# Four-step exponential, kv stage on GpSimd, 128-column q/k blocks and a four-offset convolution: one change to a fused convolution and attention kernel

## Chip, cores and metric

The kernel runs on one core of a Trainium2 chip. The metric is device time in microseconds (us), one launch per time. Lower is better. A time of a kernel that ran once has no state ("unknown"); where a kernel ran several times, a run over 1.5% above its fastest counts as slow, and ratios use the fast runs.

## The reference, cut to what matters

Two independent halves share the core; S = 2048, D = 640, bf16.

```python
# half A: short convolution, product, long causal convolution, gate
k_shift = sum over t of k_pad[:, t:t + S, :] * shift_k[:, 3 - t]
kv = k_shift * v
y = causal convolution of kv with ssm_k, length 2048, per channel   # by FFT in the reference
a = q * (y + kv * ssm_D)

# half B: attention, 32 heads of 20
qkv = x @ wqkv
p = softmax((q @ k.T) * 20 ** -0.5)
b = (p @ v) @ wo
out = concatenate([a, b], axis=-1)
```

## The kernel before

A Python planner writes one static program. It holds a clock per engine, adds an assumed cost `c` for every instruction and decides from those clocks what TensorE (PE) does next. The work is 2,048 *units* of 128x512 scores: a matmul of 20 rows writes a unit into a bank of PSUM, an exponential turns it into a tile of `P_sb`, a second matmul multiplies that by v. ScalarE (ACT) takes two or three units per instruction (a *round*); VectorE (DVE) takes single units by a bit trick.

```python
def EXP_task(k, m, vec, b0, got):              # m = 2 or 3 units
    ...
    P.op("act", lambda e: e.activation(
        P_sb[:, s0:s0 + m, :],
        PS[:, b0 * 512:(b0 + m) * 512].rearrange("p (u q) -> p u q", u=m), ACT.Exp, scale=scale),
        ...
    if vec:
        chain_start(k + m, b0 + m, got[m])

# chain_start: five DVE steps; the PSUM bank is free after the first
(lambda e: e.tensor_scalar(XI, bank[bk], scale * 1.4426950408889634 * w, 127.0 * w, op0=ALU.mult,
                           op1=ALU.add), [bkb[bk]], [bl, bh], 0.691, False),
(lambda e: e.scalar_tensor_tensor(XZ, u, w * c2 / c3, u, op0=ALU.add, op1=ALU.mult), [bl], [bz], 0.69, True),
(lambda e: e.tensor_scalar(hi, hi, 128.0, None, op0=ALU.mult), [bh], [bh], 0.456, True),
(lambda e: e.scalar_tensor_tensor(XZ, XZ, w * w * c1 / c3, u, op0=ALU.add, op1=ALU.mult), ...),
(lambda e: e.scalar_tensor_tensor(P_sb[:, z, :].bitcast(U16), XZ, 128.0 * c3 / w ** 3, hi, ...), ...)
```

The long convolution is 5,120 small matmuls (a block Toeplitz form): 16 distances `d` of 128 positions, and 8 to 128 columns in each.

```python
for d in range(16):
    for r1 in range(2):
        n = (16 - d) * 4
        ...
        lhsT = HK[sl][:, 64 + 128 * d - 32 * r1:64 + 128 * d - 32 * r1 + 128]
        rhs = sub(KVX[i], [[128, 2], [1, n]], ql * 256 + r1 * 64)     # 2n columns
        ...
        cost = max(0.025, 2 * n / 2400 + 0.0025)
```

The last thing that the planner tries when it has nothing else for PE is to multiply zeros. `P.stream` holds what PE *streams*, that is columns divided by 2.4 a nanosecond, not how long it looks busy:

```python
while P.stream and P.stream[0][0] < now - 3.4:
    P.stream.pop(0)
if sum(x[1] for x in P.stream) < ZTH and slack > 0.45 and bnow > 1:      # ZTH = 1.8
    if 0 < npv[0] % NKB:
        zeros(OBANK, 2, False)          # two matmuls of 512 zero columns
        continue
    ...
```

So zeros are added when less than 1.8 of the last 3.4 us, a share of 0.53, were streaming. Transfers are issued from SyncE; the planner books 0.43 us for each:

```python
return self.op(eng, fn, reads, writes, dsem=dsem, n=len(pairs), c=0.43 * len(pairs), kb=kb)
```

The softmax here doesn't subtract the row's maximum and nothing guards it: scores larger than these inputs give would overflow.

## Time and profile before

| | before |
|---|---|
| time, median of the first 3 runs | 893.01 us (890.0 to 896.05) |
| span of the profiled run, mean granted clock | 889.3 us, 0.987 |
| exponentials: ACT rounds of three / of two, DVE units | 419 / 310, 171 |
| convolution matmuls | 5,120, from 232.5 to 829.3 us |

The prediction shows the lines that tell what bounds it. Three more matter for what came of it: the row of the granted clock (40 slices of the span, 9 is 90% of full speed or more), the group of zero matmuls (busy us, mean ns, then the idle time before them), and ACT's wait for PE (us in all, times, longest).

```profile
PEclk9999999999699999999999999999999999999999
```

```profile
L348 PE MATMUL PS<-Zt 128*128 128x512 bf16 x208 | 63.6, 402 | 1.5 <-DVE Zt L342 1.0 <-DVE R L952 0.5
```

```profile
ACT P_sb L639 <- PE PS L597: 18.4, 24, 7.0
```

The clock is full in every slice but one. 208 zero matmuls are part of what keeps it so. ACT, which bounds the kernel, waited for PE only 18.4 us.

### The profile page before, as it was taken

The page shows a single profiled execution, that of the slowest core. Times are in us where ns is not written, and L with a number is a line of the kernel's source. Part 1 is how long each engine was busy: PE and PEld are TensorE (multiplying, and loading weights), DVE is VectorE, ACT ScalarE, POOL GpSimd, SP SyncE. Part 2 cuts the span into 40 slices and gives each one's busy share as a digit, 9 for nine tenths or more (in the row PEclk, how much of TensorE's full clock was granted, in tenths as well). Part 3 has the DMA queues.
Part 4 walks back from the last instruction along what each step waited for, and adds up shares of the span by engine and source line. Part 5 has one row for each costly group of instructions (what it writes and reads, how often), then busy time and mean ns, then how long its engine had stood idle before and what let it go on. Part 6 is the DMA issues. An engine that isn't in the chain of part 4 may idle for free.

```text
span 889.3 us, 26279 instructions
## 1 busy us (share of the span) xinstructions
PE 835.4 (94%) x11432; PEld 388.0 (44%) x11432; DVE 785.4 (88%) x1427; ACT 856.0 (96%) x737; POOL 126.5 (14%) x94
## 2 busy tenths in 40 slices
PE   9999889998999999998999999999989999999987
PEld 5432223222455554544545454444545445454322
DVE  4569999999699999998999999899999999999752
ACT  6699999999799999998999999999999999999996
POOL 3000000001522021210220220122022012200000
PEclk9999999999699999999999999999999999999999
DMA  9614233335666675553579656675644546355141
GB/s 301 202 56 153 93 116 105 105 105 90 158 176 175 176 191 140 158 138 99 161 161 180 162 162 187 177 210 146 169 131 131 163 130 190 110 162 145 32 107 56
DMA packets 83598, 129.15 MB, mean 145 GB/s; under 512 B 34561, under 2 KB 60283, under 8 KB 83483
## 3 DMA queue, kind: packets, MB, share of 16 engines
q1 hardware_dynamic: 81323, 124.36, 51.0%
q0 software_dynamic: 704, 2.74, 1.0%
q8 instruction: 90, 1.47, 0.7%
q10 hardware_dynamic: 1456, 0.37, 0.2%
q14 instruction: 25, 0.20, 0.1%
HBM read 116.81 MB, written 13.23 MB: 146 GB/s over the span
## 4 chain that ended last, share of the span: by engine, by line
ACT 48%; DVE 30%; PE 20%; issue 1%; DVEq 0%
ACT P_sb L639 48%; PE PS L931 7%; PE PS L597 6%; DVE P_sb L673 5%; DVE XI L666 5%; DVE XZ L668 5%; DVE XZ L671 5%; DVE XI L670 4%; PE PS L692 3%; PE PS L445 2%; DVE R L952 1%; PE PS L348 1%; DVE ZS L950 1%; DVE ZS L949 1%; DVE OT_sb L702 1%
## 5 line engine op out<-in xcount | busy, mean ns | idle before, releaser
L639 ACT ACTIVATE P_sb<-PS 128x1536 bf16<-128x1536 f32 (+1 forms) x729 | 851.5, 1417 | 19.1 <-PE PS L597 18.4
L597 PE MATMUL PS<-QT,KT 20*128 20x512 bf16 x2048 | 286.5, 388 | 30.6 <-ACT P_sb L639 21.7
L931 PE MATMUL PS<-R 128*128 128x128 bf16 (+15 forms) x5120 | 245.1, 194 | 3.6 <-DVE R L952 2.5
L931 PEld LDWEIGHTS PS<-R 128*128 128x128 bf16 x5120 | 197.7, 97 | 108.9 <-issue 108.5
L692 PE MATMUL PS<-P_sb,V_sb 128*21 128x512 bf16 x2048 | 173.5, 388 | 6.0 <-DVE P_sb L673 4.8
L901 POOL COPY R<-R 32x512 bf16<-32x512 bf16 x80 | 114.9, 1436 | 443.7 <-PE PS L931 431.3
L597 PEld LDWEIGHTS PS<-QT,KT 20*128 20x128 bf16 x2048 | 70.7, 91 | 200.1 <-ACT P_sb L639 153.8
L666 DVE TENSOR_SCALAR XI<-PS 128x512 int32<-128x512 f32 x171 | 117.0, 684 | 17.4 <-PE PS L597 16.8
L671 DVE SCALAR_TENSOR_TENSOR XZ<-XZ,XI 128x512 f32<-128x512 f32 x171 | 128.1, 749 | 0.0
L673 DVE SCALAR_TENSOR_TENSOR P_sb<-XZ,XI 128x512 uint16<-128x512 f32 x171 | 120.9, 707 | 4.9
L668 DVE SCALAR_TENSOR_TENSOR XZ<-XI 128x512 f32<-128x512 uint16 x171 | 123.0, 719 | 0.4
L670 DVE TENSOR_SCALAR XI<-XI 128x512 int16<-128x512 int16 x171 | 93.2, 545 | 0.0
L692 PEld LDWEIGHTS PS<-P_sb,V_sb 128*21 128x21 bf16 x2048 | 37.6, 89 | 79.4 <-issue 50.4
L348 PE MATMUL PS<-Zt 128*128 128x512 bf16 x208 | 63.6, 402 | 1.5 <-DVE Zt L342 1.0
L530 DVE TENSOR_TENSOR R<-R 128x640 bf16<-128x640 bf16 x128 | 61.6, 487 | 3.7 <-DMA R<-in_A_v_dram 0.9
L445 PE MATMUL PS<-xT,WQ 128*20 128x512 bf16 (+1 forms) x660 | 48.9, 385 | 3.6 <-DVE R L952 1.7
L445 PE MATMUL PS<-xT,R 128*20 128x512 bf16 (+2 forms) x660 | 44.8, 374 | 0.2
L702 DVE CAST OT_sb<-PS 128x512 bf16<-128x512 f32 x32 | 21.9, 685 | 14.5 <-PE PS L692 14.2
L503 PE MATMUL PS<-R,xT 128*128 128x160 bf16 (+1 forms) x240 | 31.2, 257 | 1.6 <-ACT P_sb L639 0.8
L431 DVE CAST KT<-PS 128x512 bf16<-128x512 f32 (+1 forms) x32 | 21.4, 673 | 11.1 <-PE PS L445 11.1
L878 POOL MEMSET R<- 128x2048 bf16 x2 | 3.8, 1900 | 190.7 <-DMA kvr_scratch<-R 190.6
L431 DVE CAST QT<-PS 128x512 bf16<-128x512 f32 (+1 forms) x32 | 21.6, 676 | 6.3 <-PE PS L445 6.2
(52 smaller groups left out, 302.0 us busy)
## 6 DMA issues: line engine op xcount, KB each, us to landing
R<-kext_scratch SPq DMA_DIRECT2D x640, 132.0 KB, 3.0
R<-in_A_k_dram SPq DMA_DIRECT2D x15, 640.0 KB, 3.9
kext_scratch<-in_A_ssm_k_dram POOLq DMA_DIRECT2D x1, 2560.0 KB, 14.7
R<-in_A_v_dram SPq DMA_DIRECT2D x16, 160.0 KB, 5.4
kv_scratch<-R SPq DMA_DIRECT2D x16, 160.0 KB
kvr_scratch<-R SPq DMA_DIRECT2D x16, 160.0 KB
R<-kvr_scratch SPq DMA_DIRECT2D x8, 320.0 KB, 7.0
R<-in_A_q_dram SPq DMA_DIRECT2D x32, 80.0 KB, 2.0
```

The costliest lines, as they stand in the source:

```text
L348: P.op("pe", lambda e: e.matmul(bank[bk], Zt, zrhs, start=start, stop=start, skip_group_check=True), reads=[b_Zt], writes=[bkb[bk]], tok=s ...
L445: ins = e.matmul(bank[bk][32 * i:32 * i + DH, 0:n], Wt[:, cc, off + i * DH:off + (i + 1) * DH], xT[:, cc, x0:x0 + n], start=(cc == 0), sto ...
L597: ins = e.matmul(bank[b0 + i], KT[32 * u:32 * u + DH, g, kb * 128:(kb + 1) * 128], QT[32 * u:32 * u + DH, qs(qc, g), :], start=True, stop= ...
L639: P.op("act", lambda e: e.activation(P_sb[:, s0:s0 + m, :], PS[:, b0 * 512:(b0 + m) * 512].rearrange("p (u q) -> p u q", u=m), ACT.Exp, sc ...
L666: (lambda e: e.tensor_scalar(XI, bank[bk], scale * 1.4426950408889634 * w, 127.0 * w, op0=ALU.mult, op1=ALU.add), [bkb[bk]], [bl, bh], 0.6 ...
L668: (lambda e: e.scalar_tensor_tensor(XZ, u, w * c2 / c3, u, op0=ALU.add, op1=ALU.mult), [bl], [bz], 0.69, True),
L670: (lambda e: e.tensor_scalar(hi, hi, 128.0, None, op0=ALU.mult), [bh], [bh], 0.456, True),
L671: (lambda e: e.scalar_tensor_tensor(XZ, XZ, w * w * c1 / c3, u, op0=ALU.add, op1=ALU.mult), [bl, bz], [bz], 0.69, True),
L673: (lambda e: e.scalar_tensor_tensor(P_sb[:, z, :].bitcast(U16), XZ, 128.0 * c3 / w ** 3, hi, op0=ALU.mult, op1=ALU.add), [bh, bz], [b_P[z] ...
L692: ins = e.matmul(bank[OBANK][32 * u:32 * u + DH + 1, :], V_sb[:, kb, 4 * g + u, :], P_sb[:, slot[4 * b + u], :], start=first, stop=last, t ...
L901: P.op("pool", lambda e, dst=dst, src=src: e.tensor_copy(dst, src), reads=[cv["KVr"]], writes=[cv["KVX"][i]] if X == 3 else [], extra=(cv[ ...
L931: P.op("pe", lambda e, o=o, lhsT=lhsT, rhs=rhs, st=st, last=last: e.matmul(o, lhsT, rhs, start=st, stop=last, skip_group_check=True), read ...
```

## The change

The intent is to move more exponentials from ACT to DVE. Four things give DVE room, and two relieve PE.

- The exponential on DVE becomes four steps. The q/k projections now scale the scores so that 128 is one octave (a factor of two), and an extra row of the scores matmul (11 x 2048 = 22528 = 128 x (127 + 49)) puts the exponent's offset on top. In such a word the low 16 bits are the fraction of an octave; the steps read fraction and whole word from PSUM, and the bank stays taken until the last step. The result is 2^49 too large, so ACT's exponential gets a bias of 49 ln 2 to match.
- The kv products, their four coefficient copies and half of the final products go to GpSimd.
- q and k are mostly projected in blocks of 128 columns, rounded into a staging tile, and laid out head by head through small transfers.
- The convolution uses 4 distances of 128 and splits the rest over partitions: still 5,120 matmuls, each of 26 to 32 columns.
- Constants: the zeros' target falls from 1.8 to 1.65 (a share of 0.49), and others.

```diff
-KV0, KVPACE, APACE, VQ, CONVE, ZTH, AGE, WAIT3 = 30.0, 0.75, 0.5, 3.0, 80, 1.8, 9, 0.3
+CQ = 0.0252
+KV0, KVPACE, APACE, VQ, CONVE, ZTH, AGE, WAIT3 = 30.0, 0.75, 0.5, 2.2, 60, 1.65, 9, 0.3
+NST = 2
...  exponential
-                PS[:, b0 * 512:(b0 + m) * 512].rearrange("p (u q) -> p u q", u=m), ACT.Exp, scale=scale),
+                PS[:, b0 * 512:(b0 + m) * 512].rearrange("p (u q) -> p u q", u=m), ACT.Exp, scale=LN2 / OCT, bias=SV[:, 5:6]),
...
+            u = bank[bk].bitcast(U16).rearrange("p (n h) -> p n h", h=2)[:, :, 0]
+                (lambda e: e.tensor_scalar(X, u, c3, c2, op0=ALU.mult, op1=ALU.add), [bkb[bk]], [bx], 0.691, False),
+                (lambda e: e.scalar_tensor_tensor(X, u, 0.0, X, op0=ALU.add, op1=ALU.mult), [bkb[bk], bx], [bx], 0.69, False),
+                (lambda e: e.scalar_tensor_tensor(X, X, c1, u, op0=ALU.add, op1=ALU.mult), [bkb[bk], bx], [bx], 0.69, False),
+                (lambda e: e.tensor_tensor(P_sb[:, z, :].bitcast(U16), bank[bk], X, ALU.add), [bkb[bk], bx], [b_P[z]],
+                 0.69, False)], end)
...  kv stage
-                P.op("dve", lambda e: e.tensor_tensor(o, a, b, op), reads=reads, writes=writes, c=0.486, two=True)
+                P.op("pool", lambda e: e.tensor_tensor(o, a, b, op), reads=reads, writes=writes, c=1.5)
...  q/k blocks: five rounds of 128 columns into a bank, rounded to St, then by head
+                pairs.append((dst, St[a - 128 * c:z - 128 * c, i, :]))
+            work(1, [(ev, [bkb[bk]], [b_St[i]], 0.69, False)],
+                 lambda: (P.dmas("sp", pairs, d_st[i], reads=[b_St[i]], writes=bd), st_free.append(i)))
...  convolution
-                for d in range(16):
-                    for r1 in range(2):
-                        n = (16 - d) * 4
+                for x in range(4):
+                    for k in range(8):
+                        d, r1 = divmod(k, 2)
+                        n = 16 - d
+                        rhs = sub(KVX[i], [[32, 2], [1, n]], (4 * u + x) * 64 + r1 * 16)
+                        yield (CQ, rd if x + k == 0 else [])
```

## The prediction

> **What bounds the kernel now.** The attention half needs 2,048 exponentials over units of 128x512 scores (32 heads, 16 key blocks, 4 query blocks of 512). ScalarE (ACT) does most; VectorE (DVE) does some by a five-operation bit trick. I first read the page's busy shares and its chain of waits, then the table of stretches, then the groups by shape.
>
> From the page of the kernel before, busy time by engine, then the chain that ended last:
>
> ```profile
> PE 835.4 (94%) x11432; PEld 388.0 (44%) x11432; DVE 785.4 (88%) x1427; ACT 856.0 (96%) x737; POOL 126.5 (14%) x94
> ...
> ACT 48%; DVE 30%; PE 20%; issue 1%; DVEq 0%
> ```
>
> Three engines look full. The stretches tell them apart (columns: length, then busy time of PE, weight load, DVE, ACT and GpSimd, the granted clock, DMA share, GB/s):
>
> ```profile
> 0.00:30.00 30.00, 28.03 (x370) 15.75 (x371) 14.29 (x35) 14.84 (x19) 7.87 (x12) 1.00 0.94 296
> ...
> 60.00:120.00 60.00, 55.21 (x583) 17.50 (x583) 56.52 (x115) 60.00 (x50) 0.00 (x0) 1.00 0.42 135
> ...
> 220.00:300.00 80.00, 78.05 (x1111) 40.83 (x1107) 69.28 (x114) 75.01 (x65) 23.05 (x16) 0.88 0.67 172
> 300.00:400.00 100.00, 97.19 (x1533) 50.72 (x1532) 96.57 (x160) 99.42 (x89) 21.38 (x15) 1.00 0.60 158
> ...
> 700.00:800.00 100.00, 94.97 (x1435) 49.45 (x1433) 98.11 (x166) 99.69 (x85) 17.10 (x12) 1.00 0.53 150
> ```
>
> From 30 us on ACT has hardly a gap, save 5 us in 220:300, where the clock dipped to 0.88. DVE is at 94 to 98% there too. PE is busy largely because it fills its idle time itself: 208 of its matmuls (L348) multiply zeros to keep the clock up. So the time is ACT's work, and it falls only as fast as DVE takes units away from ACT. The groups by shape give the prices:
>
> ```profile
> L639 ACT ACTIVATE P_sb<-PS 128x1536 bf16<-128x1536 f32 x419 | 607.5, 1618 | 6.0 <-PE PS L597 5.6
> L639 ACT ACTIVATE P_sb<-PS 128x1024 bf16<-128x1024 f32 x310 | 333.1, 1145 | 13.1 <-PE PS L597 12.8
> ...
> L671 DVE SCALAR_TENSOR_TENSOR XZ<-XZ,XI 128x512 f32<-128x512 f32 x171 | 128.1, 749 | 0.0
> L668 DVE SCALAR_TENSOR_TENSOR XZ<-XI 128x512 f32<-128x512 uint16 x171 | 123.0, 719 | 0.4
> L673 DVE SCALAR_TENSOR_TENSOR P_sb<-XZ,XI 128x512 uint16<-128x512 f32 x171 | 120.9, 707 | 4.9
> L666 DVE TENSOR_SCALAR XI<-PS 128x512 int32<-128x512 f32 x171 | 117.0, 684 | 17.4 <-PE PS L597 16.8
> ...
> L670 DVE TENSOR_SCALAR XI<-XI 128x512 int16<-128x512 int16 x171 | 93.2, 545 | 0.0
> ...
> L530 DVE TENSOR_TENSOR R<-R 128x640 bf16<-128x640 bf16 x128 | 61.6, 487 | 3.7 <-DMA R<-in_A_v_dram 0.9
> ```
>
> So 171 units go to DVE, and 419x3 + 310x2 = 1,877 to ACT. Neighbouring instructions overlap, so I price by start-to-start time in the trace, median: ACT 1.330 us for three units, 0.904 for two, hence 419x1.330 + 310x0.904 = 837.5 us, **0.446 us a unit**. The other 52 us of the 889.3 us span are the start (first exponential at 10.8 us), the end (last one done at 880.7) and gaps. The five DVE operations take 0.62 + 0.62 + 0.36 + 0.71 + 0.63 = **2.94 us** a unit (means). The rest of DVE's work adds up to about 269 us, of which the kv products (L530) are 61, the q/k copies 38 and the 96 final products of the convolution half 32.
>
> **What the Trainium skill says.** (1) "VectorE: DVE Perf Modes", section "Why PSUM operands drop a tier": an fp32 operand in PSUM leaves VectorE at one element per cycle. The trace agrees and shows that this costs nothing here: L666 from PSUM takes 684 ns, L668 from SBUF 719. (2) "SBUF — State Buffer", section "Who interferes with whom": a VectorE instruction with at most one SBUF input, outside the two-port modes, does not contend with GpSimd. All four new operations have at most one. In the trace the two-port candidate L670 has a median of 450 ns but a mean of 545, which fits waiting for GpSimd now. (3) "TensorE: Matmul & The Clock Gate", section "Wait — 56ns, not 53.3ns?": matmul starts are never closer than about 25 ns. The trace agrees: convolution matmuls of 8 to 40 columns start 25 ns apart (median), those of 128 columns 55. (4) "GPSIMD Engine Reference", section 3.1: about 2.6 cycles per element at 1.2 GHz, so as an estimate 1.4 us for 640 elements, plus dispatch. No two-input GpSimd operation is in this trace; a copy of 512 elements took 1.44 us.
>
> **The change part by part.**
>
> *Exponential, five steps to four.* The scores arrive in PSUM already scaled and offset by an extra row of the matmul, so DVE reads fraction and whole word there. Each step is 512 elements, about 0.69 us long (like L666), 0.60 start to start where the next operation is independent, 0.71 where it waits for the last (as L671 shows). Four steps are 2.4 us if two chains interleave, 2.75 us if none do; I take **2.62**, saving 0.32 us a unit, small because the dropped step was the cheap one (0.36).
>
> *kv stage to GpSimd.* 128 products and 4 copies, 63 us, leave DVE between 55 and 208 us, where only 5 to 8 units per 50 us went to DVE (12 to 14 later). On GpSimd, estimated at 1.5 us each, they take about 200 us and end some 20 to 40 us later than now. The convolution waits for this, but has 600 us.
>
> *Half of the final products to GpSimd.* 48 of 96: 16 us off DVE.
>
> *q/k in 128-column blocks.* 64 projections of 5 rounds become 45 (10 of the old kind, 35 new): 19 x about 1.08 us (my estimate, five times the 216 ns of a 512-column round) is 20 us off PE and 19 x 0.6 = 11 us off DVE. In exchange some 240 small DMAs lay heads out.
>
> *Convolution.* Still 5,120 matmuls, but each of 26 to 32 columns instead of 8 to 128. By the trace's pace per shape they took 171 us; at 25 to 26 ns they take about 130: 40 us off PE. The weight rows shrink from 4,224 to 1,088 bytes at the same volume. Transfers of 1,280 bytes took 55 ns (median), so 82,000 of them are about 280 us over 16 engines, against 310 us now: no new limit.
>
> *Sum.* PE's 60 us are not on the path; I count them only as fewer gaps. DVE gains: the kv stage 63/2.62 = 24 units; final products and copies 27/2.62 = 10; cheaper steps on the old 171, 171x0.32/2.62 = 21. Together 171 + 55 = 226; the shorter run takes about 4 back: **222 units on DVE, 1,826 on ACT**. Then 1,826x0.447 = 816 us (a little over 0.446, for more two-unit rounds). Start and end stay about 28 us; gaps, 24 us before, I put at 18, since the dip near 230 us may soften. 816 + 28 + 18 = 862 us span, and runs lie some 2 us above their span: about **863 us**.
>
> **Rivals.** *PSUM becomes scarce.* A scores bank used to be free after the first step; now it is held to the last. In the old trace a chain lasts 6.2 us from first start to last end (median), so about two of the seven banks for scores and side work stay taken. ACT then falls to two-unit rounds: all of them would cost 1,826x(0.452-0.446) = 11 us, and stalls might cost more: 875 to 885 us. For it: two-unit rounds have most of ACT's waiting now (12.8 of 18.4 us). Against: the new order may borrow the side bank for a chain, leaving ACT three. *The clock drops.* Short convolution matmuls move data about half of the time and the filler target is lowered. The dip at 220:300 shows what it costs: some 5 us of ACT for one slice. Repeated dips would give 875 to 895. *Late q/k or kv through DMA.* A head group that waits 3 to 5 us for its rearranged keys stalls ACT; eight such times bring 885. Against: most loads land in 2 to 6 us and are asked for well ahead. *It goes better.* If chains interleave without waits (2.45 us) and three-unit rounds dominate (0.4435), 238 units and 803 us of ACT lead to about 848.
>
> **Range and chances.** 2% faster is 875. The middle is 863; the good rival sets the low end at 848, scarce banks plus a dip the high end at 882. Faster by over 2%: 0.78; within 2%: 0.19; slower: 0.03, since ACT loses work in any case.
>
> **What would show it.** DVE units: 215 to 235 (count of the first step), each step 680 to 700 ns. ACT: about 1,826 units, still gapless from 30 us on. Convolution matmuls 25 to 26 ns apart. GpSimd products 1.4 to 1.6 us, the first convolution matmul between 240 and 280 us. Wrong if the unit count stays under 200, if a step on PSUM takes well over 0.7 us, if two-unit rounds outnumber three-unit ones by far, or if ACT waits over 40 us for PE in mid-run.

## The result and the profile after

All outputs were correct. The changed kernel took **1182.28 us** (median of 4 runs, 1177.73 to 1187.04); the kernel before took 894.53 us (median of 4, 890.0 to 912.16). The ratio of fast runs is **1.324** (95%: 1.314 to 1.334). A ratio here is the mean time of one kernel's fast runs over the mean of the other's fast runs in the same rounds, so it isn't quite the ratio of the medians. The profiled run is a fast one: the kernel is a third slower in its normal state.

The page after: busy times, the clock's row, the chain that ended last.

```profile
PE 1136.8 (97%) x10549; PEld 386.6 (33%) x10549; DVE 761.3 (65%) x1283; ACT 966.8 (82%) x858; POOL 436.7 (37%) x235
...
PEclk9995557655556555555557555555555555555558
...
PE 84%; ACT 11%; SPq 2%; DVE 2%; DMA 1%; issue 0%; DVEq 0%
```

The chain turned over: PE 20% and ACT 48% of it before, PE 84% and ACT 11% now. PE runs 883 fewer matmuls but is busy 301 us longer, because its clock is halved from the fourth slice on. The stretches show it as it happens (columns as in the prediction: length, busy PE, weight load, DVE, ACT, GpSimd, granted clock, DMA share, GB/s):

```profile
30.00:60.00 30.00, 27.17 (x302) 12.68 (x294) 17.19 (x39) 26.46 (x26) 18.38 (x15) 1.00 0.36 125
60.00:120.00 60.00, 55.19 (x294) 12.24 (x294) 40.57 (x64) 48.30 (x45) 27.69 (x20) 0.70 0.25 75
...
500.00:600.00 100.00, 99.72 (x1185) 38.96 (x1178) 69.48 (x115) 85.69 (x76) 28.79 (x6) 0.50 0.73 150
700.00:800.00 100.00, 99.22 (x1062) 35.52 (x1062) 67.92 (x111) 83.02 (x74) 48.87 (x37) 0.50 0.69 155
```

At clock 0.50 PE is busy 99 of 100 us, and ACT only 83 to 86. Both users of the scores wait for PE:

```profile
DVE X L747 <- PE PS L678: 254.0, 175, 4.8
...
ACT P_sb L720 <- PE PS L678: 190.8, 297, 6.8
```

ACT's wait for PE went from 18.4 to 190.8 us. The groups by shape answer to those of before: ACT's rounds with the bias tile `SV`, and from the page the first two of the four DVE steps and the GpSimd products.

```profile
L720 ACT ACTIVATE P_sb<-PS,SV 128x1024 bf16<-128x1024 f32 x728 | 786.6, 1117 | 165.1 <-PE PS L678 161.3
L720 ACT ACTIVATE P_sb<-PS,SV 128x1536 bf16<-128x1536 f32 x122 | 185.8, 1549 | 29.9 <-PE PS L678 29.5
```

```profile
L747 DVE TENSOR_SCALAR X<-PS 128x512 f32<-128x512 uint16 x226 | 155.9, 690 | 254.9 <-PE PS L678 254.0
...
L602 POOL TENSOR_TENSOR R<-R 128x640 bf16<-128x640 bf16 x128 | 178.7, 1396 | 126.8 <-DMA R<-in_A_v_dram 117.3
...
L748 DVE SCALAR_TENSOR_TENSOR X<-PS,X 128x512 f32<-128x512 uint16 x226 | 154.0, 683 | 2.0
```

DVE got its 226 units at the predicted step length. But ACT's rounds are now mostly of two units (728, against 122 of three), and they are dearer: 1,822 units at the closest start-to-start times of this trace (waits for PE left out), 728x0.997 + 122x1.423, are 899.4 us, against 837.5 us for 1,877 units before.

### Where the clock falls

The trace records each change of the granted clock. After the start it is 1.0 or 0.5, never between, and stretches last multiples of 3.413 us. In the kernel before it is 0.5 for two stretches, of 20.5 and 3.4 us. In the changed kernel it is full from 5.43 to 83.94 us, then half for 99 us, and later half for up to 362 us on end (633 to 995 us). PE's timeline shows what came just before the first fall (start, length, engine, line, instruction; in brackets the idle time ahead of it and what ended it), then SyncE's:

```profile
78.37 0.45 PE L575 MATMUL PS<-R,xT 128*128 128x320 bf16 x2
79.91 0.40 PE L678 MATMUL PS<-QT,KT 20*128 20x512 bf16 x4 [1.09 <-DMA KT<-St]
...
83.27 0.39 PE L678 MATMUL PS<-QT,KT 20*128 20x512 bf16 x3 [1.96 <-DVE St L562]
```

```profile
73.84 14.48 SPq L231 DMA_DIRECT2D KT<-St  x20
```

Twenty small transfers of keys took 14.48 us to issue, 0.72 each, where the planner had booked 0.43. PE waited 1.09 us for the keys and 1.96 us for a staging tile that they kept taken. Neither wait is long, but only a third of that 3.4 us window was streaming, and the clock halved at its end. A later fall, at 998.7 us, has no such cause: the clock had come back at 995.3 us, and the very next window, streaming 0.42, lost it again. The timeline of that window:

```profile
995.62 0.40 PE L769 MATMUL PS<-P_sb,V_sb 128*21 128x512 bf16 x4
996.70 0.39 PE L678 MATMUL PS<-QT,KT 20*128 20x512 bf16 x2 [0.68 <-ACT P_sb L720]
997.02 1.01 PE L1001 MATMUL PS<-R 128*128 128x32 bf16 x34
```

This is the plain rhythm of the new kernel: a two-unit round, 0.4 to 0.7 us of waiting for ACT, and 34 convolution matmuls in about a microsecond. Their starts are 25 ns apart, but 32 columns stream in 13 ns: PE looks busy and half of the time is empty. (At half clock they start 27 ns apart and stream for 22 to 27: only at full clock is the narrow convolution thin.)

To learn what decides, I counted all windows of 3.413 us, cut where the clock changes, in the 18 traces of this study (before, after and the 16 experiments). For each I worked out the share of streaming time (columns over 2.4 per ns, times the granted clock, matmuls that run side by side counted once; 512 zero columns start every 216 to 226 ns at full clock, 400 to 426 at half) and looked at the clock of the next window.

| at full clock: share | next window at half | | at half clock: share | next window at full |
|---|---|---|---|---|
| under 0.40 | 55 of 55 | | under 0.72 | 0 of 135 |
| 0.40 to 0.45 | 30 of 34 | | 0.72 to 0.80 | 4 of 655 |
| 0.45 to 0.50 | 31 of 57 | | 0.80 to 0.84 | 28 of 892 |
| 0.50 to 0.55 | 28 of 200 | | 0.84 to 0.88 | 73 of 456 |
| 0.55 and over | 2 of 2,850 | | 0.88 and over | 59 of 72 |

It is **a trap with two doors**. The clock falls when about half of a window is not streaming. It comes back after windows that stream some 85% or more, and not after all of these; below 0.84 it came back after only 32 of 1,682 windows. These counts go together with the clock; that the stream moves it is what the experiments below test. The kernel before streams 0.68 on the mean at full clock, with 11 of 250 windows under 0.55. The changed one, at full clock, streams 0.61 with 20 of 47 windows under 0.55. Once at half clock its mean share is 0.80, and 11 of 295 windows brought the clock back. The zeros' target of before, 0.53, lies just above the first door; the new one, 0.49, just below it.

### The profile page after: what moved, and what is told of

Read it like the earlier page. It is cut to its first block, busy times and chain, and to the rows that moved or that the text cites. A ratio compares the mean times of both kernels' runs of the same rounds, so it can differ in the third digit from the quotient of the medians.

```text
span 1175.9 us, 24953 instructions
## 1 busy us (share of the span) xinstructions
PE 1136.8 (97%) x10549; PEld 386.6 (33%) x10549; DVE 761.3 (65%) x1283; ACT 966.8 (82%) x858; POOL 436.7 (37%) x235
## 4 chain that ended last, share of the span: by engine, by line
PE 84%; ACT 11%; SPq 2%; DVE 2%; DMA 1%; issue 0%; DVEq 0%
PE PS L678 32%; PE PS L769 17%; PE PS L1001 14%; ACT P_sb L720 11%; PE PS L365 8%; PE PS L545 5%; PE PS L855 3%; SPq L231 2%; PE PS L575 2%; PE PS L793 1%; PE PS L463 1%; PE PS L824 1%; PE PS L881 0%; DMA R<-kext_scratch 0%; DMA KT<-St 0%
## 5 line engine op out<-in xcount | busy, mean ns | idle before, releaser
L720 ACT ACTIVATE P_sb<-PS,SV 128x1024 bf16<-128x1024 f32 (+1 forms) x850 | 961.9, 1179 | 195.0 <-PE PS L678 190.8
L678 PE MATMUL PS<-QT,KT 20*128 20x512 bf16 (+1 forms) x2048 | 480.1, 570 | 28.3 <-ACT P_sb L720 17.7
L973 POOL COPY R<-R 128x1024 bf16<-128x1024 bf16 x40 | 191.8, 4796 | 474.1 <-PE PS L1001 466.8
L747 DVE TENSOR_SCALAR X<-PS 128x512 f32<-128x512 uint16 x226 | 155.9, 690 | 254.9 <-PE PS L678 254.0
L602 POOL TENSOR_TENSOR R<-R 128x640 bf16<-128x640 bf16 x128 | 178.7, 1396 | 126.8 <-DMA R<-in_A_v_dram 117.3
L678 PEld LDWEIGHTS PS<-QT,KT 20*128 20x128 bf16 (+1 forms) x2048 | 86.0, 98 | 348.5 <-ACT P_sb L720 210.3
L1001 PE MATMUL PS<-R 128*128 128x32 bf16 (+3 forms) x5120 | 196.6, 188 | 0.4 <-DMA R<-kext_scratch 0.4
L750 DVE TENSOR_TENSOR P_sb<-PS,X 128x512 uint16<-128x512 f32 x226 | 154.7, 685 | 3.8
L749 DVE SCALAR_TENSOR_TENSOR X<-X,PS 128x512 f32<-128x512 f32 x226 | 153.9, 682 | 3.9
L748 DVE SCALAR_TENSOR_TENSOR X<-PS,X 128x512 f32<-128x512 uint16 x226 | 154.0, 683 | 2.0
```

The costliest lines, as they stand in the source:

```text
L602: P.op("pool", lambda e: e.tensor_tensor(o, a, b, op), reads=reads, writes=writes, c=1.5)
L678: ins = e.matmul(bank[bks[i]], KT[32 * u:z, g, kb * 128:(kb + 1) * 128], QT[32 * u:z, qs(qc, g), :], start=True, stop=True, tile_position= ...
L720: P.op("act", lambda e: e.activation(P_sb[:, s0:s0 + m, :], PS[:, b0 * 512:(b0 + m) * 512].rearrange("p (u q) -> p u q", u=m), ACT.Exp, sc ...
L747: (lambda e: e.tensor_scalar(X, u, c3, c2, op0=ALU.mult, op1=ALU.add), [bkb[bk]], [bx], 0.691, False),
L748: (lambda e: e.scalar_tensor_tensor(X, u, 0.0, X, op0=ALU.add, op1=ALU.mult), [bkb[bk], bx], [bx], 0.69, False),
L749: (lambda e: e.scalar_tensor_tensor(X, X, c1, u, op0=ALU.add, op1=ALU.mult), [bkb[bk], bx], [bx], 0.69, False),
```

## The experiments

**Theory.** The time is lost because the change thins PE's stream below the first door: narrow convolution, lower zeros' target, gaps for q/k, two-unit rounds. **Rivals.** Something else slows the kernel and the clock only follows: the gaps of the q/k transfers alone; the bias tile of ACT's exponential; scarce PSUM. Every experiment gave correct outputs. Those without a range are one profiled look each, of state unknown, beside one run of the kernel before on the same chip (896.17, 897.77 and 890.34 us for the first three groups, and 7 runs with a median of 892.6 for the last).

### First group: is it the stream?

**No zeros, in the kernel before.**

```diff
-... VQ, CONVE, ZTH, AGE, WAIT3 = 30.0, 0.75, 0.5, 3.0, 80, 1.8, 9, 0.3
+... VQ, CONVE, ZTH, AGE, WAIT3 = 30.0, 0.75, 0.5, 3.0, 80, 0.0, 9, 0.3
```

> The kernel before with its zero matmuls switched off (filler target 0 instead of 1.8 us of streaming per 3.4 us), nothing else. Activity theory: the clock is halved after any window of about 3.4 us in which TensorE streams columns for less than about half of the time, so without filler it must drop repeatedly: mean granted clock under 0.9, drops mainly before 220 us and after 800 us where the convolution does not fill, time over 930 us. Rival (one long gap from the q/k transfers of the changed kernel starts it, filler is irrelevant): clock 0.98, time 885 to 900 us.

Measured: 979.57 us, clock 0.836. Taking away useless work costs 83 us. The zeros are load-bearing. One detail was missed: the falls were expected before 220 and after 800 us, but half of the 20 came between.

**The narrow convolution alone, in the kernel before** (loads, layout and matmuls of the convolution as in the change; zeros' target still 1.8).

```diff
-                        n = (16 - d) * 4
+                        n = 16 - d
-                        rhs = sub(KVX[i], [[128, 2], [1, n]], ql * 256 + r1 * 64)
+                        rhs = sub(KVX[i], [[32, 2], [1, n]], (4 * u + x) * 64 + r1 * 16)
```

> The kernel before with only the convolution of the changed kernel (26 to 32 columns per matmul, filler target kept at 1.8). Activity theory: a narrow matmul takes 25 ns but streams for 11 to 13, so stretches of convolution fall under half activity: repeated drops between 220 and 830 us, mean clock 0.6 to 0.9, time 930 to 1150 us. Rival (transfer gap of the q/k projections): clock stays over 0.97, time 880 to 900 us.

Measured: 1076.99 us, clock 0.739, though nothing of the exponential, q/k or kv was touched. Its span and clock:

```profile
core 0: 1075.2 us, clock 0.739
```

The convolution streamed 1,088x320 = 348,160 columns before, 145 us at 2.4 per ns; now it is 1,280x(32+30+28+26) = 148,480, or 62 us. The planner put in more zeros (358 instead of 208), not enough. "PE saves 40 us" was true and harmful.

**The wide convolution back, in the changed kernel**, and then **the zeros' target back as well**.

```diff
-                        n = 16 - d
+                        n = (16 - d) * 4
```

```diff
-... 2.2, 60, 1.65, 9, 0.3
+... 2.2, 60, 1.8, 9, 0.3
```

> The changed kernel with the convolution of before put back (8 to 128 columns; two exponential buffers fewer to fit memory), filler target left at 1.65. Activity theory: drops remain before about 250 us and around the end, but not in the middle: mean clock 0.75 to 0.95, time 890 to 1000 us. Rival (gap at about 80 us plus a half clock from which the kernel cannot climb): as the changed kernel, clock 0.55 to 0.65, time over 1120 us.

> As e3, with the filler target of before (1.8). Activity theory: fewer drops than e3, mean clock 0.85 to 1.0, time 865 to 950 us. Rival (transfer gap and trap): still clock under 0.65 and over 1120 us.

Measured: 1127.48 us, clock 0.752, and 1129.23 us, clock 0.752. Both have the time of the rival (over 1120) and not its clock; the first has the clock of the theory (0.75 to 0.95), the second missed that too. The narrow convolution isn't the whole cause: with the old one and the old target there still were stays of 119, 99 and 253 us at half clock.

### Second group: gaps, padding, the old q/k

**Keys and queries earlier**, with four staging tiles (two fewer tiles of `P_sb` pay for them).

```diff
-NPU = 30
-NST = 2
+NPU = 28
+NST = 4
-                add(16 * max(g0, 2) + 4 * kc - 6, 1.1, ("K", c, kc), ...
+                add(16 * max(g0, 2) + 4 * kc - 16, 1.1, ("K", c, kc), ...
-                add(16 * max(g0, 2) - 7, 1.1, ("Q", c, 0), ...
+                add(16 * max(g0, 2) - 17, 1.1, ("Q", c, 0), ...
```

> The changed kernel, only with its key and query blocks asked for ten key blocks earlier and four staging tiles instead of two (and two exponential buffers fewer), so that the 20 small transfers behind the 4.6 us TensorE gap at 78 to 83 us come in time. Gap theory (this one gap throws the kernel into the half clock and it stays there): clock over 0.9, time 865 to 900 us. Activity theory (thin streaming all along is what drops the clock and keeps it from coming back): the first drop comes later or stays, but the clock is lost again by the time the convolution runs; mean clock 0.55 to 0.75, time over 1050 us.

Measured: 1167.55 us, clock 0.58. The clock fell at 85.1 us all the same. The gaps at 78 to 83 us are the first trigger, not the cause. (The "4.6 us gap" of the expectation is two waits, 1.09 and 1.96 us, with work between them.)

**Padded convolution and more zeros.** Each convolution matmul streams as many zero columns again, into a part of the bank that they don't alter (52 to 64 columns in all), at a start every 28 ns instead of 25; the zeros' target is 2.1 (a share of 0.62).

```diff
-CQ = 0.0252
-... 2.2, 60, 1.65, 9, 0.3
+CQ = 0.028
+... 2.2, 60, 2.1, 9, 0.3
-    rhs = sub(KVX[i], [[32, 2], [1, n]], (4 * u + x) * 64 + r1 * 16)
-    o = sub(bank[bk], [[256, 2], [1, n]], (4 * u + x) * 16 + d)
+    rhs = sub(KVX[i], [[(2 - i) * KVX_E - (4 * u + x) * 64, 2], [32, 2], [1, n]], (4 * u + x) * 64 + r1 * 16)
+    o = sub(bank[bk], [[128 if 4 * u + x < 8 else -128, 2], [256, 2], [1, n]], (4 * u + x) * 16 + d)
```

> The changed kernel with more streaming and no less work: each convolution matmul also streams zero columns (52 to 64 columns instead of 26 to 32, adding zeros to sums of other channels), and the filler target is 2.1 instead of 1.65. Activity theory: the drop at about 84 us stays (its gap is untouched) and lasts until a dense window comes, then the clock holds: mean clock 0.8 to 0.97, time 880 to 1000 us. Gap theory: clock lost at 84 us and not regained, under 0.65, over 1100 us.

Measured: 1072.56 us, clock 0.823. More work, 110 us less time, though the 880 to 1000 us of the theory were missed.

**Both together.**

> e5 and e6 together. Activity theory: few drops, mean clock over 0.93, time 860 to 900 us, ACT gapless as in the kernel before. Gap theory: same as e5, so no more than a few per cent from it.

Measured: 1036.28 us, clock 0.87. Both ranges of the theory were missed.

**Padding, zeros at 2.1, and q/k projected the old way** (by head groups, no staging, no small transfers).

```diff
         def own(which, g, x):
-            return g < 2 and (which == "K" or x == 0)
+            return True
```

> As e6, but with the q/k projection of before (head groups, no staging, no small transfers), which takes the gap at 80 us away by its root. Activity theory: mean clock over 0.93, time 860 to 900 us. If the clock is held and the time is still over 910 us, a second cause (bank shortage, two-unit rounds of ACT) is at work.

Measured: 1003.04 us, clock 0.907. The clock was mostly held, and the time still lay over 910, the line that I had drawn. A second cause had to be there. This stretch of it names the engine:

```profile
400.00:500.00 100.00, 92.81 (x1480) 45.36 (x1478) 87.73 (x146) 100.00 (x100) 33.80 (x7) 1.00 0.77 174
```

The clock is full, ACT is busy without a gap, and it does only 100 instructions, mostly of two units. At best, rounds of two started 997 ns apart and rounds of three 1,423, against 904 and 1,330 in the kernel before: **93 ns more each**, whatever the size. The one thing new about them is the bias tile.

### Third group: the bias tile

**No bias.** The 49 octaves come off in the last DVE step instead, which costs nothing there.

```diff
-   ... ACT.Exp, scale=LN2 / OCT, bias=SV[:, 5:6]),
+   ... ACT.Exp, scale=LN2 / OCT),
-   (lambda e: e.tensor_tensor(P_sb[:, z, :].bitcast(U16), bank[bk], X, ALU.add), ...
+   (lambda e: e.scalar_tensor_tensor(P_sb[:, z, :].bitcast(U16), bank[bk], -49.0 * OCT, X, op0=ALU.add, op1=ALU.add), ...
```

> The changed kernel, ScalarE's exponential without its bias tile; the offset of 49 octaves is taken off in the last VectorE step instead (one scalar more in the same instruction). In every trace so far two- and three-unit exponentials with the bias start 997 and 1423 ns apart at best, without it 904 and 1330. Bias theory (93 ns an instruction, and a slower ACT stretches the whole plan so that TensorE streams thinner): best start-to-start back to 904 and 1330, clock clearly up from 0.57, 0.65 to 0.9, time 950 to 1100 us. Theory that filler and narrow convolution alone keep the clock down: ACT prices fall but clock stays under 0.65 and time over 1100 us.

Measured, in the changed kernel: 1166.65 us, clock 0.570. The bias theory's ranges were missed; the other theory's (clock under 0.65, over 1100 us) were met. The start-to-start times went back to 904 and 1,330 ns, but the group shows where the gain went:

```profile
L720 ACT ACTIVATE P_sb<-PS 128x1024 bf16<-128x1024 f32 x728 | 728.1, 1033 | 212.2 <-PE PS L678 193.1
```

Busy time fell from 786.6 to 728.1 us, and the idle time before these rounds rose from 165.1 to 212.2. With PE at half clock as the bound, a faster ACT only waits more.

**No bias, in the kernel whose clock is mostly held** (the last one of the second group).

> e8 (padded convolution, filler 2.1, old q/k projection) without the bias tile: ACT prices 904 and 1330, so 861 instructions save 80 us of ACT, and TensorE's streaming per time rises by a tenth. Combined theory (bias plus thin streaming are the whole loss): clock over 0.97, time 870 to 895 us. If over 910 us with the clock held, a third cause remains.

Measured: 906.27 us, clock 0.964: 97 us less than with the bias. Of these 93x861 rounds = 80 us are the bias itself; the rest probably came with the clock (0.907 to 0.964). Above 895 us, so the range was missed; its row of the clock shows the dips, two after waits of 0.9 and 1.7 us for convolution rows, two in thin windows:

```profile
PEclk9999999999999995999998999999998599999999
```

**The bias alone, in the kernel before** (a tile of zeros as bias; nothing else changes).

```diff
-   ... ACT.Exp, scale=scale),
+   ... ACT.Exp, scale=scale, bias=ZB[:, 0:1]),
```

> The kernel before with a bias tile of zeros in the exponential, nothing else. Bias theory: 729 instructions x 93 ns = 68 us more on ACT; with the clock held 955 to 970 us; TensorE's filler was planned for a faster ACT, so some windows fall under half streaming and the clock may drop (0.8 to 0.98), then up to 1030 us. If the bias cost nothing: 890 to 900 us.

Measured: 949.79 us, clock 0.987, 59 us more than the 890.34 beside it; 729 rounds of 93 ns are 68. Slightly under the range, and the cost is plain. The groups answer to those in the prediction (1,618 and 1,145 ns on the mean there):

```profile
L641 ACT ACTIVATE P_sb<-PS,ZB 128x1536 bf16<-128x1536 f32 x419 | 680.2, 1843 | 6.1 <-PE PS L599 5.8
L641 ACT ACTIVATE P_sb<-PS,ZB 128x1024 bf16<-128x1024 f32 x310 | 392.9, 1402 | 10.0 <-PE PS L599 10.0
```

**No bias, padding, zeros at 2.1, 128-column q/k blocks kept but early.**

> e7 (padded convolution, filler 2.1, 128-column q/k blocks asked for earlier) without the bias tile: every part of the change kept but the bias. Combined theory: clock over 0.93, time 865 to 900 us. If the q/k blocks' transfers still tear gaps: clock 0.8 to 0.93, 900 to 960 us.

Measured: 1040.64 us, clock 0.82. The clock is in the range for gaps that remain, the time above it (900 to 960 us). The 128-column blocks still tear holes: PE waited up to 5.5 us for a staging tile and up to 6.9 us for convolution rows, which share the queue with the small transfers (up to 1.7 us for rows in the version without these). All 243 small transfers are issued from SyncE; at 0.72 us each, as measured for the first twenty, that is about 175 us of that queue as an estimate, where the planner booked 105.

### Fourth group: the last dips, and one part left at a time

All four start from the 906 us version (padding, zeros at 2.1, old q/k, no bias). **Transfers booked at their measured 0.72 us**, so that the planner asks for convolution rows in time (3 rounds):

```diff
-        return self.op(eng, fn, reads, writes, dsem=dsem, n=len(pairs), c=0.43 * len(pairs), kb=kb)
+        return self.op(eng, fn, reads, writes, dsem=dsem, n=len(pairs), c=0.72 * len(pairs), kb=kb)
```

> e10 with one number of its plan changed: a transfer's issue is reckoned at 0.72 us, as the traces show for the small ones, instead of 0.43, so the plan puts other work where convolution rows come late (two of e10's four drops began in a wait of 0.9 and 1.7 us for such rows). Combined theory: clock over 0.98, time 865 to 885 us, so 1 to 3% faster than before. If clock is held and it is not faster than 890, the VectorE part gains nothing even then.

Measured: fast runs of 878.5, 877.8 and 879.34 us at clock 1.0, 0.999 and 1.0; ratio to the kernel before **0.985** (0.981 to 0.989). One run, which is the profiled one, was slow: 909.63 us. Its rows of ACT's busy share and of the clock:

```profile
ACT  6699998999999999999996668999999999999996
...
PEclk9999999999999999999995557999999999999999
```

One fall, 70 to 80 us in the trap, 31 us lost. By its fast runs the version is 1.5% faster than the kernel before, which is within 2%; and it lives near the edge. PE's weight loads waited 1.5 us in all for convolution rows, against 9.7 us in the 906 us version; how much time that saved isn't shown, since that version ran only once.

**Zeros at 2.4** (3 rounds).

> e10 with the filler target 2.4 instead of 2.1. Activity theory: the two of e10's four drops that began in thin windows (ACT waits, streaming share 0.45 and 0.52) go, those that began in waits for convolution rows may stay: clock 0.96 to 1.0, time 870 to 900 us.

Measured: median 886.31 us (878.48 to 896.12), ratio of fast runs 0.987 (0.982 to 0.993). More zeros alone don't hold the clock: it was 0.971 to 0.995 in these four runs, full in none.

**The narrow convolution left in** (padding taken out), and **the zeros' target left at 1.65**.

> e10 without the padding: convolution matmuls of 26 to 32 columns again, filler 2.1, no bias, old q/k projection. If narrow matmuls count as thin streaming even beside filler: drops between 250 and 830 us, clock 0.6 to 0.85, time 960 to 1120 us. If filler alone is enough: as e10, 890 to 915 us.

> e10 with the changed kernel's filler target of 1.65 left as it is: padded convolution, no bias, old q/k projection. If the lowered target matters by itself: drops above all before 260 us, where no convolution runs, clock 0.7 to 0.93, time 930 to 1060 us. If not: as e10, 890 to 915 us.

Measured: 1080.25 us, clock 0.693, and 1021.73 us, clock 0.803, both in the expected ranges; but in the second most falls came after 260 us, where few were expected.

The sets of runs side by side:

| part | alone in the kernel before (about 893) | alone put back into the 906 us version | alone taken out of the change (1182) |
|---|---|---|---|
| narrow convolution | 1077 | 1080 | 1127 |
| zeros' target 1.65 | 980 (target 0) | 1022 | not run |
| 128-column q/k blocks | not run | 1041 (early ones) | not run (1168 for early ones) |
| bias tile | 950 | 1003 | 1167 |

Each part alone costs 59 to 184 us where the clock is mostly held. Taken out of the finished change, none brings back more than 55 us, because the others keep the clock down. The parts don't add: the four surcharges on 906 are 174 + 115 + 134 + 97 = 520 us, and the whole of them together cost 276. Most cells are single looks, and runs of one version lay up to 31 us apart (878 to 910), so the 14 or 16 us between 1182 and 1168 or 1167 mean nothing.

## Why the prediction was wrong, point by point

**What held.** DVE took 226 units (222 predicted). The four steps last 690, 683, 682 and 685 ns (680 to 700 predicted), and start 608, 715, 721 and 608 ns after each other (medians), 2.65 us a unit for the 2.62 taken. GpSimd's products take 1,396 ns (1.4 to 1.6 us). Convolution matmuls start 25 ns apart. Of the signs listed as "wrong if", two came: two-unit rounds outnumber the others six to one, and ACT waited 190.8 us for PE.

**The step that failed: "PE's 60 us are not on the path; I count them only as fewer gaps."** PE was not on the path, but its streaming was what kept its clock. The kernel before, at a mean share of 0.68, stood 0.13 of a window above the upper edge of the door (0.55), with zeros to hold it there. I had read those zeros as filler, noted that they keep the clock up, and then booked the narrower convolution (83 us less of streaming) and 20 us less of projection as relief, and left the lower target to a rival. The runs show the opposite: narrow convolution alone, 893 to 1077; no zeros, 893 to 980.

**The rival "the clock drops" was named and sized wrongly.** It put one dip at 5 us of ACT and repeated ones at 875 to 895 us. That came from the one dip in the kernel before, where 20 us at half clock cost little. It took for granted that the clock comes back when the thin stretch is over. It does not: the windows that left mostly streamed 0.84 or more, and the changed kernel at half clock streamed 0.80 on the mean and stayed there for hundreds of us. The share of half-clock time, not the number of falls, sets the price.

**ACT's price of 0.447 us a unit failed for a cost that stood in the diff.** The bias is one keyword in it, and I gave it no line. It is 93 ns a round, 850 rounds, 79 us. The Trainium skill states it, in "ScalarE: Activation LUTs", section "What ACT_TABLE_LOAD costs": each `[128,1]` pointer operand adds about 93 ns. The traces agree within a nanosecond: 904 to 996, 1,330 to 1,423 with the bias alone. ACT's price was 899.4/1,822 = 0.494 us a unit. So "ACT loses work in any case", on which the 0.03 for "slower" rested, was false: ACT got 62 us more. Even a clock held at 1.0 would have given about 950 us as an estimate: these 899.4 us of ACT and the 51 us of start, end and gaps that remain in the version with the booked 0.72 us (that sum stands below).

**"PSUM becomes scarce" came true in count, and its own price was nearly right.** 728 of 850 rounds hold two units. In the version with the booked 0.72 us, whose clock held in its fast runs, 757 two-unit and 106 three-unit rounds at 0.904 and 1.330 are 825 us for 1,832 units, against 816 predicted. That they also thin PE's stream, since PE waits for ACT in each, is argued from the timeline above and not tested by itself.

**"Late q/k through DMA" came true as the first trigger.** I priced a wait of 3 to 5 us as such; here waits of 1.1 and 2.0 us were enough, because they fell into one window. They were a trigger only: without them the clock fell at 85.1 us.

**kv later on GpSimd, and the convolution's rows.** The first convolution matmul started at 378 us, not 240 to 280: the products waited 117 us for loads of v, and the run was at half clock. In the run with the booked 0.72 us it is 282 us, near the range. The 81,920 packets of rows took 71 ns each (median), 387 us over 16 engines where I had estimated 280: a third more, still hidden.

**The sum with the clock held.** Without the bias, with padding and more zeros and the old q/k, the sum of the prediction is about right: the span of the fast runs, 876 us, less 825 us of ACT leaves 51 for start, end and gaps (46 predicted); the time is 878 us against 863. Without the bias the arithmetic of ACT and DVE was sound; the clock that it stood on wasn't. Two slips in the working change little: by the lines that it shows, start and end are 10.8 + 8.6 = 19.4 us, not 28 (the 52 us with the gaps stand), and the good rival's terms, 803 + 28 + 18 + 2, are 851, not 848.

**Open.** Streamed columns separate the windows, but the share of the array's area in use (a 20-row matmul fills less of it) separates them about as well, at 0.30 to 0.33; the runs don't decide. Thirteen of 72 half-clock windows at 0.88 and over stayed at half, unexplained. The kv stage on GpSimd alone and the 128-column blocks alone were not run in the kernel before, and PSUM held to the last step was tested nowhere by itself.

## What to carry to other kernels

Before counting less work on an engine as gain, ask whether that work holds up a clock: sum the *streamed columns* per 3.4 us window, not the busy time, and keep every window well above a half, because in these traces a fall cost not one window but all those until one streamed some 85% or more. Narrow matmuls 25 ns apart looked busy and streamed half; padding them with zero columns was worth 174 us here (1080 against 906). And price each new operand in a diff, a bias tile as well as an instruction.

## What the Trainium skill lacked or had wrong

- "TensorE: Matmul & The Clock Gate", Part 1: two clock states and a window of 3,413 ns are as stated (only 1.0 and 0.5 occur, in multiples of 3.41 us). Its advice to avoid idle gaps over about 3.4 us is too weak for this case (it does say that frequent micro-idles make the clock swing, without a measure): in the changed kernel it first fell with no gap over 2.0 us; in all traces it falls when a window streamed under about half (85 of 89 windows under 0.45, 2 of 2,850 at 0.55 or more).
- The same part puts the return after one busy window. Here a window must stream some 85%: 59 of 72 at 0.88 and over returned, 73 of 456 at 0.84 to 0.88, 4 of 790 under 0.80, with stays of up to 362 us in the changed kernel and 505 us without its bias. The part has the spacing of narrow matmuls (32 columns every 25 ns, 13.3 ns of array time, as here), but no word that to the clock they count as half a stream, as the table above has them.
- "ScalarE: Activation LUTs", section "What ACT_TABLE_LOAD costs": right within a nanosecond (93 ns for a bias tile), but stated under a heading where one looks for table loads.
- No page has a measured time on this chip for issuing small transfers in a row from SyncE ("DMA: Bandwidth & Descriptors" has only a count of sequencer cycles for "previous generations"): here 0.72 us each, 14.48 us for twenty.
